# Linear attention and a Strassen-like MLP on one core: order at the changes of chunk, loads spread out, a last transpose on TensorE

## The chip, the core and the metric

The program runs on one core of a Trainium2 chip. The metric is the device time of one execution in microseconds (us). A core has five instruction streams that run beside each other and meet at semaphores: TensorE (PE, with its weight loads PEld), VectorE (DVE), ScalarE (ACT), GpSimd (POOL) and SyncE (SP), which here only issues transfers (SPq in the views is its queue). Each stream is executed in order, so an instruction that waits holds up all that stand behind it.

## What is computed

```
phi(x)  = exp(h - max h) / sqrt(128),  h = (x*s) @ omega.T - |x*s|^2/2
x       = phi(q) @ (phi(k).T @ v) / (phi(q) @ sum phi(k) + 1e-6)   # 8 batches, 8 heads, 576 x 64
u       = x + (x.T @ U @ V).T                                       # x as 8 x 576 x 512, rank 32
out     = u + relu(u @ w1) @ w2                                     # 512 -> 2048 -> 512
```

All of it is in float32. For precision each factor of a product of the MLP is split into a high part (rounded to the matmul's own float type) and a low part (what the rounding lost), and three passes are summed: high*high, high*low, low*high.

## The kernel before

The program has two halves. The first, up to some 306 us, is the attention and the rank-32 mixing; it leaves u in DRAM. The second is the MLP over 36 tiles of 128 rows, six to a **chunk** (768 rows), so six chunks, 0 to 5. Chunk 0 is computed plainly. Chunk 1 uses seven products in place of eight for the first matrix product (`products`). Chunks 2 to 5 do so for both (`products2` and `Group`).

**A pair.** The 2048 hidden columns go in eight pairs `p` = 0 to 7. In a pair, `product(i)` for i = 0 to 6 is six matmuls of 384 columns, summed in one of two PSUM banks: X for even i, Y for odd i. After product i, `after(i)` lists copies and sums that combine the seven into hidden values, apply the relu and split them. A step of the schedule is one i, and n = 7p + i counts 0 to 55 through a chunk. The next pair takes the same two banks with the names exchanged: its product 0 writes the old Y, its product 1 the old X. So product 1 of a pair waits until everything that reads X in step 6 of the pair before is done. The last reader of X is the low part of its relu, `less(T[2] ...)` at line 1063 (chunks 2 to 5), or the second instruction of `relu` at line 999 (chunk 1).

**The second product.** From pair 2 of chunk 2 on, each step also has on PE a block of the second matrix product of the two pairs before (`Group.block(s)`, line 1293, s = 0 to 13 over two pairs), six matmuls, whose result `evict` adds on DVE to a sum in SBUF (line 816). In chunks 0 and 1 the second product is plain (line 1136), its matmuls put between the products by `take`.

**Order.** Nearly all of the second half is pinned to the order in which the code issues it (`keep`). `between(i)` issues, after each step, the transfers (`feed` loads the weights `wx` of the products six steps ahead, `group.load` and `done.load` those `wy` of the second product) and the preparation of the next chunk by `forward`: `fetch` loads a quarter of 128 columns of u (96 KB, line 376), `turn` transposes 32x32 blocks on DVE into `w1f` (line 952), `prepare` forms the four sums of blocks (the fourth on POOL, line 816, the others on DVE, line 806), `add` copies one operand to its high part on ACT (line 978) and puts its low part (DVE, line 806) into `later`, from where `lowers()` issues it one step later. In chunk 1, `new.add` and `pairs.add` prepare the weights of the next pair (lines 806, 809, 813) and `seconds` those of the second product (`wa`, `wb`, `wt`, lines 806, 816, 897, 898). `stores` holds the additions of u and the writes of the plain second product (lines 1162, 1163). `leave` writes the chunk before out: `turn_out` transposes a quarter on DVE, `write_out` (line 1322) stores it in 128-byte pieces. At the end of the program `end` does the same for the last chunk.

## Time and profile before

| | |
|---|---|
| runs | 1071.74, 1068.39, 1064.89 us; median 1068.39 |
| profiled execution | 1066.96 us, its span from first to last instruction 1065.2 us |
| PE busy | 1036.5 us, 97% of the span |
| DVE, ACT, POOL busy | 785.2, 600.8, 478.5 us |
| mean granted TensorE clock | 0.995 of full speed |
| DMA | 226.45 MB, mean 213 GB/s; 326720 of 389027 packets under 512 bytes |

PE is busy nearly all the time, so only the moments at which it stands still, and the end, are of interest. A bracket behind a row gives the idle time of the row's engine just before it, and what ended it. The second half begins at about 440 us (chunk 1), 574 us (chunk 2), and then a chunk every 118 us.

### The profile page before, as it was taken

To read this page: it belongs to the slowest core of one execution; us is meant where nothing else is said; L and a number is where in the kernel's file an instruction comes from. 1 tells how busy PE (TensorE), PEld (TensorE's weight loads), DVE (VectorE), ACT (ScalarE), POOL (GpSimd) and SP (SyncE) were. 2 spreads that over 40 slices of the span, in tenths; PEclk is the share of its full clock that TensorE was granted. 3 is DMA by queue.
4 is the path that set the end of the run, shared out by engine and by line. 5 is a ranking of instruction groups with operands and counts; after the bars stand their busy time and mean duration, and the time that the engine had idled before them with its cause. 6 is when DMAs were issued, how large, how long until landed. Compare 5 with 4: busy or idle time off the path is not lost.

```text
span 1065.2 us, 19235 instructions
## 1 busy us (share of the span) xinstructions
PE 1036.5 (97%) x6447; PEld 990.4 (93%) x6447; DVE 785.2 (74%) x1546; ACT 600.8 (56%) x1497; POOL 478.5 (45%) x419
## 2 busy tenths in 40 slices
PE   8999999999999999999998999999999999999996
PEld 7899999999989999889887999999999999999995
DVE  4798998998977776576766567776678667876555
ACT  5889989998856664444444433543445333543430
POOL 3346537557445555477863323422334223433221
PEclk9999999999999999999999999999999999999998
DMA  9899989788224475298877999789997999888886
GB/s 136 145 164 146 181 178 165 154 179 131 90 78 151 146 161 98 91 321 267 260 249 266 317 242 284 250 262 283 283 302 246 284 272 306 251 267 273 256 230 139
DMA packets 389027, 226.45 MB, mean 213 GB/s; under 512 B 326720, under 2 KB 341056, under 8 KB 388928
## 3 DMA queue, kind: packets, MB, share of 16 engines
q1 hardware_dynamic: 380160, 224.13, 80.6%
q10 hardware_dynamic: 8768, 1.08, 0.7%
q8 instruction: 52, 0.85, 0.4%
q14 instruction: 47, 0.39, 0.1%
HBM read 176.91 MB, written 48.23 MB: 211 GB/s over the span
## 4 chain that ended last, share of the span: by engine, by line
PE 86%; DVE 7%; ACT 3%; DMA 2%; issue 1%; POOL 1%; DVEq 0%; SPq 0%; ACTq 0%; POOLq 0%
PE p_s L1017 24%; PE p_c L1293 11%; PE p_o L1293 6%; PE p_p L990 6%; PE p_kv L486 4%; PE p_n L532 4%; PE p_n L1136 4%; PE p_q L1136 4%; PE p_p L574 3%; PE p_r L1293 3%; PE p_p L575 3%; PE p_p L576 3%; PE p_q L512 2%; PE py L346 2%; PE p_kv L1136 2%; PE p_m L1136 2%
## 5 line engine op out<-in xcount | busy, mean ns | idle before, releaser
L1017 PE MATMUL p_s<-ux,wx 128*128 128x384 f32 x1680 | 338.9, 337 | 8.8 <-DVE t L1063 6.4
L1017 PEld LDWEIGHTS p_s<-ux,wx 128*128 128x128 f32 x1680 | 297.9, 189 | 17.3 <-DVE t L1063 8.0
L589 ACT ACTIVATE e<-p_p,nm 128x128 f32<-128x128 f32 x576 | 167.0, 389 | 24.1 <-DVE nm L582 15.8
L1293 PE MATMUL p_c<-t,wy 128*128 128x384 f32 x768 | 153.6, 335 | 3.3 <-DVE w1f L816 1.9
L816 POOL TENSOR_TENSOR near<-b,near 128x384 f32<-128x384 f32 x32 | 42.6, 1331 | 252.4 <-DVE near L1063 252.4
L436 POOL TENSOR_TENSOR xl<-xT,xh 128x384 fp32r<-128x384 f32 x95 | 94.1, 1010 | 112.9 <-ACT xh L432 91.6
L1293 PEld LDWEIGHTS p_c<-t,wy 128*128 128x128 f32 x768 | 134.6, 188 | 5.2 <-DVE w1f L816 3.2
L582 DVE TENSOR_REDUCE nm<-p_p 128x4 f32<-128x512 f32 x144 | 97.9, 680 | 23.2 <-PE p_p L576 12.7
L1073 ACT CAST t<-near 128x768 fp32r<-128x768 f32 x64 | 53.6, 838 | 95.9 <-DVE near L1063 82.3
L574 PE MATMUL p_p<-omh,xh 128*128 128x256 f32 x288 | 92.7, 322 | 1.1 <-ACT e L589 0.9
L816 DVE TENSOR_TENSOR near<-p_s,near 128x384 f32<-128x384 f32 x88 | 48.7, 553 | 46.9 <-PE p_s L1017 42.7
L575 PE MATMUL p_p<-oml,xh 128*128 128x256 f32 x288 | 81.6, 283 | 0.0
L576 PE MATMUL p_p<-omh,xl 128*128 128x256 f32 x288 | 81.5, 284 | 0.0
L1293 PE MATMUL p_o<-t,wy 128*128 128x384 f32 x384 | 76.5, 334 | 0.0
L816 POOL TENSOR_TENSOR t<-near,t 128x768 fp32r<-128x768 f32 x32 | 61.7, 1930 | 31.2 <-ACT t L1073 31.2
L532 PE MATMUL p_n<-kv,eT 128*128 128x65 f32 x512 | 71.3, 269 | 0.1
L990 PE MATMUL p_p<-ux,wx 128*128 128x384 f32 x384 | 70.7, 335 | 0.0
L532 PEld LDWEIGHTS p_n<-kv,eT 128*128 128x128 f32 x512 | 67.1, 192 | 2.3 <-DVE x L557 0.3
L990 PEld LDWEIGHTS p_p<-ux,wx 128*128 128x128 f32 x384 | 67.6, 188 | 1.6
L1293 PEld LDWEIGHTS p_o<-t,wy 128*128 128x128 f32 x384 | 67.5, 188 | 0.0
L486 PE MATMUL p_kv<-vt,e 128*128 128x65 f32 x480 | 66.3, 262 | 0.6 <-ACT e L589 0.6
L183 POOL TENSOR_TENSOR mag<-mag,low 128x512 int32<-128x512 int32 (+2 forms) x35 | 45.3, 1295 | 46.2 <-DVE mag L161 42.6
(176 smaller groups left out, 2244.6 us busy)
## 6 DMA issues: line engine op xcount, KB each, us to landing
wx<-wx_dram SPq DMA_DIRECT2D x112, 512.0 KB, 4.7
wy<-w2x_dram SPq DMA_DIRECT2D x112, 512.0 KB, 5.2
raw<-in_moe_w_ch_dram SPq DMA_DIRECT2D x32, 512.0 KB, 4.3
wx_dram<-wx SPq DMA_DIRECT2D x56, 256.0 KB, 2.4
u_dram<-x SPq DMA_DIRECT2D x36, 256.0 KB, 2.2
qt<-in_q_dram SPq DMA_DIRECT2D x120, 72.0 KB, 2.9
uraw<-u_dram SPq DMA_DIRECT2D x80, 96.0 KB, 6.5
kt<-in_k_dram SPq DMA_DIRECT2D x52, 144.0 KB, 5.0
```

The costliest lines, as they stand in the source:

```text
L486: tc.keep_in_program_order(nc.tensor.matmul(o, e[:, j, :], w, start=(s == 0 and j == 0), stop=(s == NT - 1), skip_group_check=True))
L532: nc.tensor.matmul(pn[:, h, :], eT[:, h, :], kv[:, h, s // 5, :], start=True, stop=True)
L574: nc.tensor.matmul(o, part.xh[g][:, ts], oh, start=True, stop=False)
L575: nc.tensor.matmul(o, part.xh[g][:, ts], ol, start=False, stop=False)
L576: nc.tensor.matmul(o, part.xl[g][:, ts], oh, start=False, stop=True)
L582: nc.vector.tensor_reduce(out=self.nm[:, :n], in_=self.pp[:, :n], axis=AX.X, op=ALU.max, negate=True)
L589: nc.scalar.activation(out=self.e[:, j, :], in_=self.pp[:, j, :], func=AF.Exp, bias=self.nm[:, j : j + 1])
L816: keep(engine.tensor_tensor(out=out, in0=a, in1=b, op=op))
L990: keep(nc.tensor.matmul(ph, l, r, start=(cc + i == 0), stop=(cc == NC - 1 and i == 2)))
L1017: keep(nc.tensor.matmul(o, l, r, start=(i in (0, 1, 3) and k + j == 0), stop=(k == 1 and j == 2), skip_group_check=True,))
L1136: keep(nc.tensor.matmul(po, l, r, start=(begin and n + i == 0), stop=(end and n == len(fs) - 1 and i == 2)))
L1293: keep(nc.tensor.matmul(bank, l, r, start=(fresh and n + m == 0), stop=(n == 1 and m == 2), skip_group_check=True,))
```

## The change

It is made of five parts. (1) In `products2` the low part of X's relu and its reader come ahead of the copy and the sum of the double tile `t75`, on ACT and on DVE, and behind the eviction of the step's block. (2) In `products` the low parts of the relus go into a list and are issued a step later, behind the sum of that step; at step 6, behind `between(6)`. (3) At the changes of chunk the `add`s, the `prepare`s and the weight sums are dealt out over other steps. (4) The loads of u for a chunk are issued every second step, the first half of them in the chunk before the one before; the outputs leave in quarter tiles of 48 KB from four rooms that are used twice a chunk. (5) At the end, the last two quarters are transposed by TensorE, copied out of PSUM by ACT and DVE, and stored in pieces of 1 KB by six transfers of SP. The core of the diff:

```diff
     def relu(self, x, due=None):
         g = gp.tile([P, 2, HT], F32R, name="g", bufs=6)
         keep(nc.scalar.activation(out=g[:, 0], in_=x, func=AF.Relu))
-        keep(nc.vector.scalar_tensor_tensor(
+        step = lambda: keep(nc.vector.scalar_tensor_tensor(
             out=g[:, 1], in0=x, scalar=0.0, in1=f32(g[:, 0]), op0=ALU.max, op1=ALU.subtract
         ))
+        step() if due is None else due.append(step)
...
         for i in range(7):                                     # products
             self.product(i, w(i), (X, Y))
             take(steps, spread[i])
+            old = len(due)
             after(i)
+            for _ in range(old):
+                due.pop(0)()
             lowers()
             between(i)
+        for step in due:
+            step()
...
             elif i == 5:                                       # products2
                 sums(c12, Y, u2, ADD)
                 flush()
                 less(c22, c12, c22)
                 less(c12, c12, b11)
                 sums(two[0], b11, c22, SUBTRACT, nc.gpsimd)
-                due.append(both(7, 5, c_2, nc.vector))
             elif i == 6:
                 keep(nc.scalar.activation(out=two[1], in_=X, func=AF.Relu))
                 one(2, X)
-                flush()
+                due.append(both(7, 5, c_2, nc.vector))
...
             evict()
-            if i < 5:
-                for _ in range(early_due):
-                    due.pop(0)()
+            for _ in range(early_due if i < 5 else len(due)):
+                due.pop(0)()
...
             while nxt.made < NC:                               # end of chunk 0
                 nxt.add()
                 lowers()
+            nxt.prepare(4)
...
+    SECOND = (
+        tuple(b + a for b in (8, 16, 22, 28) for a in range(4)), (15, 21, 27, 33), (36, 37, 43), tuple(range(49, 56)),
+    )
...
-                    if i == 0:                                 # chunk 1
+                    if i in (0, 1, 2):
+                        now.add()
+                    if i == 2:
                         pairs.add()
-                    if i == 1:
-                        now.prepare(4)
-                    if i in (0, 2, 3):
-                        now.add()
-                for _ in range((0, 0, 0, 1, 2, 2, 2)[i] if p == 0 else 1):
+                if p == 1 and i < 3:
+                    pairs.add()
+                for _ in range((0, 0, 0, 1, 1, 1, 1)[i] if p == 0 else (0, 1, 1, 1, 1, 1, 2)[i] if p == 1 else 1):
                     if new:
                         new.add()
...
-                forward(nxt, n, ((8, 16, 22, 28), (15, 21, 27, 33), (36, 38, 40), (50, 51, 52, 53, 54, 55)))
-                if n == 53:
+                forward(nxt, n, SECOND)
+                if n == 52:
                     nxt.prepare(4)
...
-    ADDS, REST = (50, 51, 52, 55), (0, 1, 2)
+    EARLY_U = (46, 48, 50, 52, 54, 56, 58, 60)
+    LATE_U = tuple(range(24, 40, 2))
+    TURNS, SUMS, ADDS, REST = (22, 23, 36, 44), (25, 45, 46), (49, 50, 51, 55), (0, 1, 2)
+    OUT_A = {8: (2, 0), 9: (2, 1), 10: (3, 0), 11: (3, 1)}
+    OUT_B = {21: (4, 0), 24: (4, 1), 28: (5, 0), 32: (5, 1)}
+    WRITE_B = (29, 31, 33, 34, 36, 38, 40, 41, 43, 45, 47, 48, 50, 52, 54, 55)
...
-                    forward(nxt, n, ((20, 24, 30, 34), (29, 33, 38, 42), (35, 43, 44), ADDS))
-                    if n == 53:
+                    forward(nxt, n, (LATE_U, TURNS, SUMS, ADDS))
+                    if n == 52:
                         nxt.prepare(4)
+                    if c == 2 and n in range(4, 20, 2):
+                        nxt.fetch((n // 2 - 2 & 3,))
+                    elif c > 2 and n + 56 in EARLY_U:
+                        nxt.fetch((EARLY_U.index(n + 56) % 4,))
+                if second_next and n in EARLY_U:
+                    second_next.fetch((EARLY_U.index(n) % 4,))
...
+                if n in OUT_A or n in OUT_B:                   # leave
+                    k = (*OUT_A, *OUT_B).index(n)
+                    ys[k] = half_room(k % 4)
+                    turn_out(c - 1, *(OUT_A.get(n) or OUT_B[n]), ys[k])
+                k, a = divmod(n - 12, 4)
+                if 0 <= k < 4:
+                    write_out(c - 1, 2 + k // 2, k % 2, a, ys[k])
...
+    last = [half_room(2 + j) for j in range(2)]                # the end
     for s in range(14):
...
+        if s > 11:
+            done.evict(4, j, parted(done.banks[1, j]), parted(last[j]))
...
+    for half in (1, 0):
+        y = dec.tile([P, 2 * DM], F32, name="near", tag="raw", bufs=RB)[:, :TOK].rearrange("p (t m) -> p t m", t=3)
+        for t in range(3):
+            po = ps.tile([P, 2 * P], F32, name="p_t", tag="p_p", bufs=2)
+            for j in range(2):
+                x = sum_of(NCH - 1, 5, j).rearrange("p a b -> p (a b)") if half else last[j]
+                keep(nc.tensor.transpose(po[:, j * P : (j + 1) * P], x[:, t * P : (t + 1) * P], ident))
+            if (t + half) % 2:
+                keep(nc.scalar.copy(out=y[:, t], in_=po))
+            else:
+                keep(nc.vector.tensor_copy(out=y[:, t], in_=po))
+            r = first[NCH - 1] * P + half * HT + t * P
+            keep(nc.sync.dma_start(out=rows_out[r : r + P, 2 * P :], in_=y[:, t]))
```

How the instructions stand, at three places. First, DVE at the end of pair 0 of chunk 2 (`near` are the copies and sums in SBUF, `t_8124` is t75, `t_8133` the low part of X's relu). Before:

```order
L816 TENSOR_TENSOR near<-p_s,near 128x384 x2
L1063 SCALAR_TENSOR_TENSOR t_8109<-near,t_8109 128x384
L1063 SCALAR_TENSOR_TENSOR near<-near 128x384
L1063 SCALAR_TENSOR_TENSOR near<-near,b_8012 128x384
L816 TENSOR_TENSOR t_8124<-near,t_8124 128x2x384
L1063 SCALAR_TENSOR_TENSOR t_8133<-p_s,t_8133 128x384
L1162 TENSOR_TENSOR u<-p_q,u 128x512
```

With the change, at the same place:

```order
L816 TENSOR_TENSOR near<-p_s,near 128x384 x2
L1069 SCALAR_TENSOR_TENSOR t_8109<-near,t_8109 128x384
L1069 SCALAR_TENSOR_TENSOR near<-near 128x384
L1069 SCALAR_TENSOR_TENSOR near<-near,b_8014 128x384
L1069 SCALAR_TENSOR_TENSOR t_8133<-p_s,t_8133 128x384
L816 TENSOR_TENSOR t_8135<-near,t_8135 128x2x384
L1166 TENSOR_TENSOR u<-p_q,u 128x512
```

The reader of X (`<-p_s`) has moved one row up, past the subtraction of t75, which needs ACT's copy of `near`.

Second, DVE at the end of pair 3 of chunk 1 (`g<-p_s` is the last reader of X there). Before:

```order
L816 TENSOR_TENSOR near<-p_s,near 128x384
L999 SCALAR_TENSOR_TENSOR g<-near,g 128x384
L999 SCALAR_TENSOR_TENSOR g<-p_s,g 128x384
L806 SCALAR_TENSOR_TENSOR wt<-wa,wb 128x256
L806 SCALAR_TENSOR_TENSOR wt<-wt,wa 128x256
L952 STREAM_TRANSPOSE w1f<-uraw 128x384 x2
```

With the change:

```order
L816 TENSOR_TENSOR near<-p_s,near 128x384
L999 SCALAR_TENSOR_TENSOR g<-near,g 128x384 x2
L806 SCALAR_TENSOR_TENSOR wt<-wa,wb 128x256
L806 SCALAR_TENSOR_TENSOR wt<-wt,wa 128x256
L952 STREAM_TRANSPOSE w1f<-uraw 128x384 x2
L999 SCALAR_TENSOR_TENSOR g<-p_s,g 128x384
```

Here the reader of X has moved down, past two sums of weights and two transposes.

Third, SP in pairs 0 and 1 of chunk 2. Before:

```order
L1353 DMA wx<-wx_dram 128x1024 x2
L1163 DMA out_dram<-u 128x512
L1353 DMA wx<-wx_dram 128x1024
L1275 DMA wy<-w2x_dram_5402 128x1024
L1163 DMA out_dram<-u 128x512
```

With the change:

```order
L1361 DMA wx<-wx_dram 128x1024
L376 DMA uraw<-u_dram_69 32x24x32
L1361 DMA wx<-wx_dram 128x1024
L1167 DMA out_dram<-u 128x512
L376 DMA uraw<-u_dram_69 32x24x32
L1361 DMA wx<-wx_dram 128x1024
L1280 DMA wy<-w2x_dram_5402 128x1024
L376 DMA uraw<-u_dram_69 32x24x32
```

A load of u has come in at every second step, between the loads of weights.

## Rows read from the trace of the kernel before

**Rows 1.** PE's waits: engine, line, for whom; us in total, times, longest us.
```profile
PE p_s L1017 <- DVE t L1063: 6.4, 5, 2.8
PE p_c L1293 <- DVE w1f L816: 1.9, 4, 1.0
PE p_s L1017 <- DVE ux L806: 1.1, 1, 1.1
PE p_s L1017 <- DVE g L999: 1.1, 1, 1.1
PE p_n L1136 <- ACT g L998: 0.9, 1, 0.9
```
**Rows 2.** Windows: us, busy us (count) of PE, PEld, DVE, ACT, POOL; clock, DMA share, GB/s.
```profile
586.00:590.00 4.00, 4.00 (x16) 4.00 (x17) 1.75 (x4) 2.36 (x4) 1.97 (x2) 0.61 0.67 202
590.00:594.00 4.00, 4.00 (x24) 3.95 (x23) 2.29 (x5) 1.53 (x3) 0.00 (x0) 0.97 0.92 296
640.00:660.00 20.00, 18.34 (x103) 17.38 (x102) 13.23 (x25) 7.62 (x15) 8.28 (x5) 1.00 1.12 253
660.00:680.00 20.00, 20.00 (x118) 20.00 (x117) 13.16 (x23) 10.08 (x18) 4.51 (x3) 1.00 0.89 318
680.00:700.00 20.00, 19.10 (x109) 18.46 (x108) 17.94 (x28) 9.75 (x17) 6.70 (x4) 1.00 0.71 230
```
**Rows 3.** Timeline at the end of pair 3 of chunk 1: start, us, engine, instruction.
```profile
501.08 0.56 DVE L999 SCALAR_TENSOR_TENSOR g<-p_s,g 128x384 fp32r<-128x384 f32 x1 [0.29 <-ACT g L998]
...
502.68 0.94 DVE L806 SCALAR_TENSOR_TENSOR wt<-wa,wb 128x256 f32<-128x256 f32 x1 [1.03 <-POOL wb L816]
...
503.89 1.23 PE L1017 MATMUL p_s<-ux,wx 128*128 128x384 f32 x6
...
504.43 1.03 DVE L952 STREAM_TRANSPOSE w1f<-uraw 128x384 f32<-128x384 f32 x2
```
**Rows 4.** Timeline at the ends of pairs 0 and 1 of chunk 2.
```profile
582.88 0.56 DVE L1063 SCALAR_TENSOR_TENSOR near<-near,b 128x384 f32<-128x384 f32 x1
...
583.47 0.83 ACT L1073 CAST t<-near 128x768 fp32r<-128x768 f32 x1 [1.81 <-DVE near L1063]
...
584.84 1.31 POOL L816 TENSOR_TENSOR near<-near 128x384 f32<-128x384 f32 x1 [0.54 <-ACT near L1100]
...
585.21 0.55 DVE L1063 SCALAR_TENSOR_TENSOR t<-p_s,t 128x384 fp32r<-128x384 f32 x1
585.68 0.68 DVE L1162 TENSOR_TENSOR u<-p_q,u 128x512 f32<-128x512 f32 x1
...
585.82 9.16 PE L1017 MATMUL p_s<-ux,wx 128*128 128x384 f32 x42 [2.80 <-DVE t L1063]
...
586.83 0.37 SPq L1353 DMA_DIRECT2D wx<-wx_dram  x1
...
597.79 1.31 PE L1017 MATMUL p_s<-ux,wx 128*128 128x384 f32 x6 [1.77 <-DVE t L1063]
```
**Rows 5.** All loads of wx (L1353): from issue to landing.
```profile
DMA to landing us min/median/max: 3.4/4.7/10.7
```
**Rows 6.** Timeline at the change from chunk 2 to 3.
```profile
683.22 1.84 POOL L816 TENSOR_TENSOR w1f<-w1f 128x768 f32<-128x768 f32 x1 [7.28 <-DVE ux L806]
683.52 1.95 DVE L1063 SCALAR_TENSOR_TENSOR t<-near,t 128x384 fp32r<-128x384 f32 x1
```
**Rows 7.** Timeline of the end.
```profile
1041.69 1.32 PE L1293 MATMUL p_c<-t,wy 128*128 128x384 f32 x6 [0.98 <-DVE w1f L816]
...
1051.18 4.33 PE L1293 MATMUL p_c<-t,wy 128*128 128x384 f32 x24
...
1056.85 5.75 ACTq L1322 DMA_DIRECT2D out_dram<-yh  x8
```
**Rows 8.** All stores of line 1322: from issue to landing.
```profile
DMA to landing us min/median/max: 1.7/4.7/8.2
```
**Rows 9.** The attention's transposes on PE (L512): ns min/median/max, first and last start.
```profile
L512 PE MATMUL p_q<-ident,e x288: 270/273/332, 30.8 to 303.3; 128*128 128x128 f32 x144
```

More of the change, by code (lines that the diff above doesn't have):

```diff
@@ L994, in whole1, with relu @@
             return g
-        def relu(self, x):
+        def relu(self, x, due=None):
             g = gp.tile([P, 2, HT], F32R, name="g", bufs=6)
             keep(nc.scalar.activation(out=g[:, 0], in_=x, func=AF.Relu))
-            keep(nc.vector.scalar_tensor_tensor(
+            step = lambda: keep(nc.vector.scalar_tensor_tensor(
                 out=g[:, 1], in0=x, scalar=0.0, in1=f32(g[:, 0]), op0=ALU.max, op1=ALU.subtract
             ))
+            step() if due is None else due.append(step)
             return g
@@ L1025, in products @@
             y5, c11, _ = self.room()
-            g = {}
+            g, due = {}, []
             def after(i):
@@ L1032, in after @@
                     sums(c11, Y, p1, ADD)
-                    g[0, 0] = self.relu(c11)
+                    g[0, 0] = self.relu(c11, due)
                 elif i == 2:
@@ L1039, in after @@
                     sums(c22, X, y5, ADD)
-                    g[1, 1] = self.relu(c22)
+                    g[1, 1] = self.relu(c22, due)
                 elif i == 5:
                     sums(c12, Y, u2, ADD)
-                    g[0, 1] = self.relu(c12)
+                    g[0, 1] = self.relu(c12, due)
                 elif i == 6:
-                    g[1, 0] = self.relu(X)
+                    g[1, 0] = self.relu(X, due)
             for i in range(7):
@@ L1296, in block, with evict @@
             return lambda: self.evict(i, j, parted(bank))
-        def evict(self, i, j, bank):
+        def evict(self, i, j, bank, to=None):
             if i == 2 and self.g < LAST:
@@ L1305, in evict @@
             else:
-                sums(a, bank, a, ADD)
+                sums(to or a, bank, a, ADD)
     def turn_out(c, i, j, y):
@@ L1333, in forward @@
     def forward(new, n, at):
-        base, turn, prepare, add = at
-        for j, b in enumerate(base):
-            if b <= n < b + 4:
-                new.fetch((n - b,))
+        pieces, turn, prepare, add = at
+        if n in pieces:
+            new.fetch((pieces.index(n) % 4,))
         if n in turn:
@@ L1354, in feed @@
             wq[q], wq[q + 1] = pair[:, 0], pair[:, 1]
+    chunks = {c: Chunk(c) for c in range(2, NCH)}
     for c in range(1, 2):
-        now, nxt = nxt, Chunk(c + 1)
+        now, nxt = nxt, chunks[2]
         second_weights = (None for p in range(NH) for _ in seconds(p))
@@ L1393, in performer_mlp_kernel @@
             steps = now.second([p, p + NH], g, p == 0, p == NH - 1)
-    ADDS, REST = (50, 51, 52, 55), (0, 1, 2)
+    EARLY_U = (46, 48, 50, 52, 54, 56, 58, 60)
[4 more added lines that the diff above has]
+    WRITE_B = (29, 31, 33, 34, 36, 38, 40, 41, 43, 45, 47, 48, 50, 52, 54, 55)
     pend, done = [], None
     for c in range(2, NCH):
-        now, nxt = nxt, Chunk(c + 1) if c + 1 < NCH else None
+        now, nxt, second_next = chunks[c], chunks.get(c + 1), chunks.get(c + 2)
         now.res, ys = {}, {}
@@ L1422, in between @@
                         stores.pop(0)()
-                    if n == 0:
-                        now.add()
                 elif n in REST:
@@ L1429, in between @@
                 if nxt:
[L1430 to L1431 removed]
+                    forward(nxt, n, (LATE_U, TURNS, SUMS, ADDS))
+                    if n == 52:
                         nxt.prepare(4)
[L1434 to L1449 removed]
+                    if c == 2 and n in range(4, 20, 2):
[4 more added lines that the diff above has]
+                    second_next.fetch((EARLY_U.index(n) % 4,))
+            def leave(n):
+                if n in OUT_A or n in OUT_B:
[5 more added lines that the diff above has]
+                    write_out(c - 1, 2 + k // 2, k % 2, a, ys[k])
+                if n in WRITE_B:
+                    k, a = divmod(WRITE_B.index(n), 4)
+                    write_out(c - 1, 4 + k // 2, k % 2, a, ys[4 + k])
             at = 7 * NH * (c - 2) + 7 * p
@@ L1463, in end @@
             write_out(NCH - 1, i, j, a, y, nc.scalar if j else nc.sync)
-    ys = {}
+    last = [half_room(2 + j) for j in range(2)]
     for s in range(14):
-        done.block(s)()
+        bank = done.block(s)
+        j = s % 2
+        if s > 11:
+            done.evict(4, j, parted(done.banks[1, j]), parted(last[j]))
+        else:
+            bank()
         done.load(s)
-        j = s % 2
         if s in (6, 7):
-            ys[j] = whole_room()
-            end(2, j, ys[j][:, :HT])
-        elif s in (10, 11):
-            end(3, j, ys[j][:, HT:])
-        elif s > 11:
-            end(5, j, half_room(j))
-    for j in range(2):
-        end(4, j, half_room(2 + j))
+            end(2, j, half_room(j))
+        elif s in (9, 10):
+            end(3, 1 - j, whole_room()[:, :HT])
+    for half in (1, 0):
[7 more added lines that the diff above has]
+                keep(nc.scalar.copy(out=y[:, t], in_=po))
+            else:
+                keep(nc.vector.tensor_copy(out=y[:, t], in_=po))
+            r = first[NCH - 1] * P + half * HT + t * P
+            keep(nc.sync.dma_start(out=rows_out[r : r + P, 2 * P :], in_=y[:, t]))
 _INS = ['q', 'k', 'v', 'omega', 'moe_U', 'moe_V', 'moe_w_ch1', 'moe_w_ch2']
```

15 lines of the change are left out of this document (removed).

## The prediction

> **What bounds the kernel now.** The page comes first: PE is busy 97% of the span at a clock of 0.995, so a gain can only come from the moments at which PE stands still, and from the end, where it has nothing left. The view of PE's waits [rows 1] names them in the second half; five of these groups add up to 11.4 us. The windows [rows 2] tell what a wait really costs. An undisturbed stretch of 20 us holds 118 matmuls, 0.17 us each; the stretch with a change of chunk holds 109. Nine are missing, 1.5 us, while PE's idle time there is only 0.9 us in two waits (20.00 less 19.10). So I add 0.3 us to each wait that a row shows, for the pipeline that fills again. The timelines [rows 3, 4, 6, 7] then show, wait by wait, what ended last. In chunks 2 to 5 it is nearly always the same thing: bank X is released by the low part of its relu, and that stands on DVE behind other work.
>
> **The change, place by place.** Minus is a gain.
>
> *Start of chunk 1: -2.6.* PE waited 1.1 us for a low part of an operand (`ux`) and 0.9 us for a relu on ACT that stood behind copies of weights [rows 1]; with 0.3 each, 2.6. With the change the fourth sum is issued at the end of chunk 0, the three last operands at steps 0, 1 and 2, so each low part lies at least two steps ahead of its product, and four copies of weights have left this pair. ACT's copy of the seventh operand still has to wait for POOL. Bounds 0 and -2.6; I take the upper gain, as two steps are more than the wait was.
>
> *Ends of pairs 3, 4 and 5 of chunk 1: +2.1, +1.0, -1.4.* By the second order shown, the reader of X at the end of pair 3 now stands behind two `wt` sums and two transposes. The first `wt` could not start before 502.68, since POOL's sum `wb` ended then, and the second transpose ended at 505.46 (504.43 + 1.03); another 0.56 us for the reader gives 506.0. PE began product 1 of the next pair at 503.89 [rows 3]: 2.1 us of new waiting. Bounds: 0 if the `wb` sum comes that much earlier, 2.4 with the filling pipeline. At the end of pair 4 two shorter `wt` sums stand in front; between 0 and 2.1 I take half, 1.0. At the end of pair 5 a sum of blocks leaves the queue ahead of the reader, and with it the wait of 1.1 us for `g` [rows 1], 1.4 with the filling; bounds 0 and -1.4.
>
> *Ends of pairs 0 and 1 of chunk 2: -4.0.* No blocks of the second product stand between the pairs yet, so nothing covers the chain. Before, DVE ended its last `near` at 583.44, ACT then copied t75 (to 584.30), DVE subtracted, and only then read X, from 585.21; PE went on at 585.82 [rows 4]. With the change the reader follows `near` at once: 583.45 to 584.0, so PE goes on some 1.8 us earlier. The long wait also lowered the clock: after those 2.80 us the window 586 to 590 shows 0.61 of full speed (the lower level, 1.2 in place of 2.4 GHz, for most of it) and 16 matmuls, where the next 4 us hold 24 [rows 2]: 8 x 0.17 = 1.4 us. After the wait of 1.77 us at 597.79 nothing like that is seen, and 1.0 us is left of the first wait, so I count the 1.4 as gained. The second wait, 1.77, goes almost wholly: -1.8. Against that, +1.0: SP issues the weights of step 14 only after the store of u at step 6, which waits for DVE's addition (585.68 to 586.36), and then at 586.83 [rows 4]. DVE's queue there is no shorter than it was, but PE now reaches step 14 at about 590.3 (584.0 and six products of 1.04), 3.5 us later, while these loads take 3.4 to 10.7 us, 4.7 in the median [rows 5]. 4.7 - 3.5 gives 1.2, with the load of u ahead in the queue or not; bounds 0 and 2.4; I take 1.0.
>
> *640 to 660 us, chunk 2: -2.2.* 103 matmuls in place of 118 at a DMA share of 1.12, with 1.66 us of idle time [rows 2]. The quarters of u were loaded there in every step, between the weights on SP's queue; now it is every second step, and half of them earlier. Bounds: 0, and 15 x 0.17 = 2.5 (some of the missing matmuls may be missing records).
>
> *Three changes of chunk: -4.5.* Each loses 1.5 us (one window of the three stands in [rows 2]). Two things delay the reader of X there, and both move. A low part of an operand is issued between the sums of steps 4 and 5; it now comes a step earlier. And DVE's low part at 683.52 took 1.95 us instead of 0.56, since POOL's sum in `w1f` ran from 683.22 to 685.06 [rows 6]: DVE got nothing done until POOL was through. That sum now starts a step, 2.1 us, earlier, so it ends before DVE comes to this instruction. I expect X to be free 0.9 us before PE asks: from the end of product 5, DVE needs 0.57 x 4, then the eviction of step 5, that of step 6, which cannot start before 3.1 us, and the reader, 4.3 in all; PE asks at 5 x 1.04 = 5.2. Bounds 0 and -4.5.
>
> *Before the last group: -1.3.* PE waited 0.98 us for an eviction that stood behind t75 and the reader [rows 7]; it now stands ahead of both.
>
> *The end: -3.7.* PE's last matmul ends at 1055.51 and ACT's eight last stores are issued from 1056.85 on, until 1062.60 [rows 7]; the last begins half a microsecond before that, at 1062.1. With the change six pieces pass through two PSUM banks: two transposes (0.27 us each as the attention's [rows 9], overlapping, so 0.4) and a copy of some 0.45 us (0.56 for 384 columns, here 256), ACT and DVE in turn. Two pieces per 0.95 us, three rounds: 2.85, so the last transfer is issued at 1058.4 by SP, which has done its other stores by then. Both kinds of store land in 1.7 us at best [rows 8], so the landing cancels: 1058.4 - 1062.1 = -3.7. Bounds -2.7 and -4.7: a third of a round per bank slower, or landings of the larger pieces at the shortest seen.
>
> *At nothing:* the smaller output tiles. The bytes stay, SP issues eight more stores per chunk at some 0.4 us, and it waits most of a step anyway; if that slack went, weights six steps ahead would come late first.
>
> **Here the trace and a page are weighed.** ACT's copy of t75 ended at 584.30 and POOL started its second subtraction at 584.84, held up by ACT's relu of X [rows 4]. That relu now comes first, so POOL may start at the same moment as DVE's subtraction of t75, and the rows leave open who is first; I count no wait. The Trainium skill (SBUF - State Buffer, section "Who interferes with whom") says that a DVE instruction with two SBUF inputs and a GpSimd instruction that reads SBUF exclude each other for the whole instruction, and that the one issued first goes first. The trace agrees on DVE's side, with the 1.95 us above; POOL's 1.31 us at 584.84 show no delay behind DVE's. By that rule alone the sum would be 1.2 us less of a gain.
>
> **Sum.** -2.6 + 2.1 + 1.0 - 1.4 - 4.0 - 2.2 - 4.5 - 1.3 - 3.7 = -16.6. From the profiled 1066.96 that is 1050.4; the median of the runs, 1068.39, lies 1.4 above the profiled one, so I forecast **1051.8**. With the gains at their upper bounds and the new waits at 0 it is 5.1 lower (2.1 + 1.0 + 1.0 + 1.0), 1046.7; with both new waits of chunk 1 at 2.1, the late weights at 2.4, and nothing gained at 640 us, at pair 5 and at one of the last two places, 1057.9.
>
> **Rivals.** (a) *DVE meets POOL at every pair.* If POOL goes first in all 32 pairs, t75 ends up to 1.3 us later. Mostly the 0.9 us of slack and the next step cover it, since the reader of X is through by then; at pair 0 of chunk 2 it delays the addition, the store and so the weights of step 14: +1.2, and some tenths elsewhere, **1053.4**. For it: the two become ready within 0.05 us. Against: t75 is read by PE only steps later. (b) *The reader of X is now held by the eviction.* It stands behind the eviction of step 6, and that waits for PE's block. If DVE's queue is longer than I count (it was busy 17.94 of 20 us at the change of chunk [rows 2]), the 0.9 us are used up and the gains of the three changes and of the last group stay out, 5.8: **1057.6**. (c) *New waits eat more.* If the wait at pair 3 is long enough to lower the clock (+1.4), pair 4 costs 2.1, the weights of step 14 come 2.4 us late and the stretch at 640 us gains nothing: 1.4 + 1.1 + 1.4 + 2.2 more, **1058**. (d) *Slower: the four output rooms.* Each is used twice a chunk; DVE's transpose into it waits for the stores of its first use, whose last is issued 6 steps earlier (12.5 us) in one case and 5 steps (10.4 us) in three. Stores land in 4.7 us in the median, 8.2 at most [rows 8]. Were they to need over 10.4 us, counted from the step, DVE would stand, X would stay taken, and each us beyond 0.9 would cost PE one, twelve times over chunks 3 to 5: at 13.6 us, 12 x 2.3 = 27 us, **1079**. Against it: SP keeps in step with PE, and the load on DMA is spread.
>
> **Chances.** About 1% is what this measurement can tell from no change, 10.7 us here: faster means below 1057.7. Forecast 0.58 (nearly all faster), (a) 0.14 (nearly all faster), (b) 0.12 and (c) 0.12 (each somewhat under half faster, the rest the same), (d) 0.04. That gives faster 0.78, same 0.17, slower 0.05. The range reaches from the forecast's low bound, 1046, to 1060, which takes in (a) to (c) with a little for the spread of the runs.
>
> **What would show it.** Right: the group `p_s <- DVE t L1063` of PE's waits falls from 6.4 us to about 1; the windows at the three changes hold 117 or 118 matmuls; the clock stays up at pair 0 of chunk 2; the last transfer is issued some 3 us after the last product. Wrong: new waits of PE for `g` at the ends of pairs 3 and 4 of chunk 1 of more than 3 us together (c); waits for `wx` or `wy` in chunk 2 (c); `p_s <- DVE t` after the eviction of step 6 (b); DVE idle ahead of a transpose into `yh`, ended by a DMA (d). The forecast fails as a whole if PE's matmuls per 20 us fall below 117 in stretches that were undisturbed.

## The result and the profile after

The changed kernel takes **1055.16 us** (median of 6 runs, 1053.24 to 1056.55), the kernel before beside it 1066.62 (6 runs): a ratio of 0.9887, 95% interval 0.986 to 0.9914. That is 11.5 us less; 16.6 were forecast. The profiled executions, 1066.96 and 1055.76 us, differ by 11.2, so they can be compared place by place. The table does it by the starts of the same products on PE in both timelines: how much each place made the gap larger or smaller. Minus is a gain; each measured row is rounded by itself, so the rows add up to -11.4.

| place | forecast, us | measured, us |
|---|---|---|
| everything up to the start of chunk 1 | 0 | +2.1 |
| start of chunk 1 | -2.6 | -1.6 |
| ends of pairs 3, 4, 5 of chunk 1 | +2.1, +1.0, -1.4 | +1.5, -0.1, -1.4 |
| end of pair 7 of chunk 1 | 0 | +0.7 |
| pairs 0 and 1 of chunk 2, up to step 17 | -4.0 | -1.5 |
| 640 to 660 us | -2.2 | -2.4 |
| three changes of chunk | -4.5 | -4.4 |
| before the last group | -1.3 | -1.3 |
| after the last product | -3.7 | -3.0 |
| sum | -16.6 | -11.2 |

PE's longest waits from chunk 1 on, in the columns of [rows 1] (the reader of X is at line 1069 now, `p_t` are the transposes of the end):

```profile
PE p_s L1018 <- DVE g L999: 2.2, 2, 1.3
...
PE p_s L1018 <- DVE t L1069: 0.9, 1, 0.9
...
PE p_t L1498 <- DVE near L1502: 0.8, 2, 0.5
PE p_s L1018 <- DVE b L816: 0.8, 1, 0.8
PE p_s L1018 <- ACT t L1079: 0.8, 1, 0.8
PE p_s L1018 <- ACT near L1090: 0.7, 1, 0.7
```

The 6.4 us for the reader of X are down to 0.9. Four groups for `p_s` add up to 4.5: three are new, and the one for `g`, 1.1 us at the end of pair 5 before, now stands for the ends of pairs 0 and 3. The windows, in the columns of [rows 2]:

```profile
586.00:590.00 4.00, 3.21 (x17) 2.57 (x16) 2.31 (x4) 2.44 (x6) 3.06 (x2) 1.00 0.43 100
...
640.00:660.00 20.00, 20.00 (x117) 20.00 (x116) 12.99 (x24) 8.80 (x17) 6.72 (x5) 1.00 0.96 280
680.00:700.00 20.00, 20.00 (x117) 20.00 (x116) 17.98 (x29) 11.26 (x21) 6.94 (x6) 1.00 0.98 277
```

The change of chunk and the stretch at 640 us are full now: 117 matmuls, where [rows 2] hold 109 and 103. At 586 to 590 us the granted clock stays at full speed, and yet only 17 matmuls pass, one more than at 0.61 before: PE now waits there. At the change of chunk, against [rows 6]:

```profile
678.56 1.85 POOL L816 TENSOR_TENSOR w1f<-w1f 128x768 f32<-128x768 f32 x1 [5.64 <-DVE ux L806]
...
680.65 0.55 DVE L1069 SCALAR_TENSOR_TENSOR t<-near,t 128x384 fp32r<-128x384 f32 x1
...
683.77 0.55 DVE L1069 SCALAR_TENSOR_TENSOR t<-p_s,t 128x384 fp32r<-128x384 f32 x1
...
685.18 1.20 PE L1018 MATMUL p_s<-ux,wx 128*128 128x384 f32 x6
```

POOL's sum is over before DVE needs the time (0.55 in place of 1.95 us), X is free at 684.32, and PE comes to it at 685.18 without a wait, 0.86 us later; 0.9 were forecast. The end of pair 3 of chunk 1, against [rows 3]:

```profile
502.50 0.94 DVE L806 SCALAR_TENSOR_TENSOR wt<-wa,wb 128x256 f32<-128x256 f32 x1 [1.19 <-POOL wb L816]
...
504.41 1.04 DVE L952 STREAM_TRANSPOSE w1f<-uraw 128x384 f32<-128x384 f32 x2
...
505.38 0.52 DVE L999 SCALAR_TENSOR_TENSOR g<-p_s,g 128x384 fp32r<-128x384 f32 x1
...
505.95 1.32 PE L1018 MATMUL p_s<-ux,wx 128*128 128x384 f32 x6 [1.30 <-DVE g L999]
```

The new wait is there, behind two sums and two transposes, as the order said. And pairs 0 and 1 of chunk 2, against [rows 4]:

```profile
584.68 0.55 DVE L1069 SCALAR_TENSOR_TENSOR t<-p_s,t 128x384 fp32r<-128x384 f32 x1
...
585.29 3.77 PE L1018 MATMUL p_s<-ux,wx 128*128 128x384 f32 x18 [0.94 <-DVE t L1069]
...
585.66 0.96 DVE L816 TENSOR_TENSOR t<-near,t 128x768 fp32r<-128x768 f32 x1 [0.43 <-ACT t L1079]
585.71 1.79 POOL L816 TENSOR_TENSOR near<-near 128x384 f32<-128x384 f32 x1
586.54 0.68 DVE L1166 TENSOR_TENSOR u<-p_q,u 128x512 f32<-128x512 f32 x1
587.14 0.55 DVE L816 TENSOR_TENSOR b<-p_s,near 128x384 f32<-128x384 f32 x1
587.25 0.34 SPq L1167 DMA_DIRECT2D out_dram<-u  x1
...
591.74 0.39 SPq L1361 DMA_DIRECT2D wx<-wx_dram  x1
...
598.36 1.28 PE L1018 MATMUL p_s<-ux,wx 128*128 128x384 f32 x6 [0.77 <-ACT t L1079]
...
600.80 0.56 DVE L816 TENSOR_TENSOR acc<-p_c,w1f 128x384 f32<-128x384 f32 x1 [3.65 <-DMA out_dram<-u]
601.27 0.55 DVE L816 TENSOR_TENSOR b<-p_s,near 128x384 f32<-128x384 f32 x1
```

SP issued weights at 582.29 and then stood until 587.25, since the store of step 6 waits for DVE's addition (586.54 to 587.22). The weights of step 16 went out at 591.74 and took 6.5 us, to 598.2: PE's wait at 598.36 is put down to an ACT instruction that ended then, but it fits the weights, and in the first experiment below the same wait is put down to them. At 600.80 DVE had stood 3.65 us at the first eviction, whose room is that of a tile of u. The chain of waits names the store (start, us, what):

```profile
593.23 7.47 DMA out_dram<-u
```

Behind that eviction stood the sum that reads bank Y, and PE got step 17 only at 601.87. The end, against [rows 7]:

```profile
1042.94 4.33 PE L1298 MATMUL p_c<-t,wy 128*128 128x384 f32 x24
...
1045.31 3.04 ACTq L1327 DMA_DIRECT2D out_dram<-uraw  x4
...
1047.78 0.41 DVE L1502 COPY near<-p_t 128x256 f32<-128x256 f32 x1
...
1048.39 0.70 ACT L1500 COPY near<-p_t 128x256 f32<-128x256 f32 x2 [13.71 <-DVE near L1502]
...
1048.79 2.79 SPq L1504 DMA_DIRECT2D out_dram<-near  x6
...
1050.32 0.42 DVE L1502 COPY near<-p_t 128x256 f32<-128x256 f32 x1 [0.53 <-PE p_t L1498]
```

The first of the six pieces is copied by ACT. Its wait is put down to a copy on DVE, but ACT issues stores of an earlier quarter until 1048.35 (1045.31 + 3.04), and its copy begins at 1048.39; PE's first four transposes had ended by 1047.70. SP issues its first piece when this copy is done, and then one about every 0.48 us.

### The profile page after: what moved, and what is told of

Read it like the earlier page. It is cut to its first block, busy times and chain, and to the rows that moved or that the text cites. A ratio compares the mean times of both kernels' runs of the same rounds, so it can differ in the third digit from the quotient of the medians.

```text
span 1054.0 us, 19271 instructions
## 1 busy us (share of the span) xinstructions
PE 1036.1 (98%) x6459; PEld 991.5 (94%) x6459; DVE 785.9 (75%) x1543; ACT 598.9 (57%) x1500; POOL 466.0 (44%) x419
## 4 chain that ended last, share of the span: by engine, by line
PE 85%; DVE 5%; DMA 3%; ACT 2%; SPq 2%; issue 1%; POOL 1%; ACTq 0%; DVEq 0%; POOLq 0%
PE p_s L1018 25%; PE p_c L1298 12%; PE p_p L990 6%; PE p_o L1298 6%; PE p_n L532 4%; PE p_kv L486 4%; PE p_n L1140 4%; PE p_q L1140 4%; PE p_r L1298 3%; PE p_p L574 3%; PE p_q L512 2%; PE p_p L575 2%; PE p_p L576 2%; PE py L346 2%; PE p_kv L1140 2%; PE p_m L1140 2%
## 5 line engine op out<-in xcount | busy, mean ns | idle before, releaser
L816 POOL TENSOR_TENSOR t<-near,t 128x768 fp32r<-128x768 f32 x32 | 59.1, 1848 | 38.9 <-ACT t L1079 38.9
L486 PEld LDWEIGHTS p_kv<-vt,e 128*128 128x128 f32 x480 | 63.4, 191 | 1.6 <-ACT e L589 1.5
```

The source lines that it names most:

```text
L486: tc.keep_in_program_order(nc.tensor.matmul(o, e[:, j, :], w, start=(s == 0 and j == 0), stop=(s == NT - 1), skip_group_check=True))
L816: keep(engine.tensor_tensor(out=out, in0=a, in1=b, op=op))
```

## Experiments

All medians stand beside runs of the kernel before on the same chip (medians 1065.98 to 1067.69 us). The kernels were not all run beside each other, so they are compared by their ratios to the kernel before, with the 95% interval behind, or by the stages; the intervals of the relus at once and of the last four kernels of the table overlap, so what parts these five is read from the stages. "After" is the changed kernel. The stages below, in us, are read from each kernel's profiled execution, again by the starts of products.

| kernel | start of chunk 1 | chunk 1 | chunk 2, steps 8-20 | steps 34-48 | chunk 3 to 4 | from chunk 1 to the end |
|---|---|---|---|---|---|---|
| before | 439.9 | 126.3 | 22.5 | 31.6 | 117.9 | 625.3 |
| after | 442.1 | 124.8 | 22.9 | 29.1 | 116.5 | 611.9 |
| after, again | 440.8 | 124.8 | 23.0 | 29.1 | 116.5 | 611.6 |
| relus at once | 440.5 | 122.7 | 22.9 | 29.1 | 116.5 | 609.9 |
| u as before | 441.4 | 124.8 | 22.0 | 30.1 | 116.5 | 612.3 |
| u at 14 to 21 | 439.7 | 124.9 | 20.8 | 29.1 | 116.5 | 614.0 |
| readers only | 440.0 | 126.0 | 21.8 | 32.0 | 117.6 | 620.7 |
| sum earlier | 440.3 | 126.1 | 23.0 | 29.5 | 116.5 | 621.6 |
| u spread, chunk 2 | 440.1 | 126.1 | 22.5 | 29.1 | 117.9 | 622.5 |
| store later | 440.1 | 122.9 | 20.8 | 29.1 | 116.5 | 608.1 |
| other rooms | 439.0 | 123.1 | 21.0 | 29.1 | 116.5 | 608.3 |
| reader first | 439.9 | 122.7 | 20.6 | 29.1 | 116.5 | 606.8 |
| half early | 439.3 | 122.9 | 20.9 | 29.1 | 116.5 | 607.9 |

**The relus at once** (after, one edit in `products`):

```diff
-                for _ in range(old):
+                for _ in range(old if i < 6 else len(due)):
                     due.pop(0)()
...
-            for step in due:
-                step()
```

> The changed kernel, but in chunk 1 the last low part (the reader of X) is issued straight behind step 6, ahead of the sums and transposes of that step. Theory: three waits of PE for g, at the ends of pairs 0, 3 and 7 of chunk 1, come from the reader standing behind that work; they go, 0.9 + 1.5 + 0.6 = 3.0 us, so about 1052 us, and the rows of PE's waits for g at line 999 fall from 5.9 us to under 1.5. Rival: DVE is held by POOL's sums and copies in those places whatever the order; then the waits only change their place, 1055 us.

1050.79 us, ratio 0.9857 (0.9839 to 0.9874). The waits for `g` at line 999 are gone. At the end of pair 3:

```profile
499.60 0.55 DVE L999 SCALAR_TENSOR_TENSOR g<-p_s,g 128x384 fp32r<-128x384 f32 x1
...
500.86 0.94 DVE L806 SCALAR_TENSOR_TENSOR wt<-wa,wb 128x256 f32<-128x256 f32 x1 [0.72 <-POOL wb L816]
```

The reader runs in the time in which DVE waits for POOL. Pair 0 gave 0.92, pair 3 1.47, pair 7 0.37 us: this part of the change cost time, and its undoing beats the change; its four runs (1049.51 to 1052.13) all lie below those of the change. Chunk 2 is that of the change, and here the profile puts PE's wait at step 16 down to the weights, which landed at 594.04:

```profile
594.17 1.28 PE L1018 MATMUL p_s<-ux,wx 128*128 128x384 f32 x6 [0.60 <-DMA wx<-wx_dram]
```

**Loads of u as before** (after, `forward` of chunk 2 on with the steps of before, no early loads):

```diff
-                    forward(nxt, n, (LATE_U, TURNS, SUMS, ADDS))
+                    forward(nxt, n, (ALL_U, (29, 33, 38, 42), (35, 43, 44), ADDS))
...
-                if second_next and n in EARLY_U:
-                    second_next.fetch((EARLY_U.index(n) % 4,))
```

> The changed kernel with the loads of u, the transposes and three of the sums for the next chunk back at the steps of the kernel before (no loads at steps 4 to 18 of chunk 2, none in the chunk before). Theory: the waits at steps 16 and 17 of chunk 2 (0.96 us for late weights, 1.44 us for a sum behind the late store of u) come from the eight early loads of u in that stretch; they go (-2.4), and the 2.4 us at 640 to 660 us come back: 1055 us in all, with the loss in the other place. Rival: the weights and the store are late because PE now reaches those steps 3.5 us earlier, with or without the loads; then the waits stay and the loss at 640 to 660 us is added: 1057.6 us.

1052.92, ratio 0.9889 (0.9863 to 0.9915); one of its six runs, 1060.46, lies far above the others and weighs in the ratio. Neither theory: of the waits at steps 16 and 17 only 1.0 of 2.4 us went, and of the loss at 640 us only 1.0 came back.

**Loads of u at steps 14 to 21 of chunk 2** (after):

```diff
-                    if c == 2 and n in range(4, 20, 2):
-                        nxt.fetch((n // 2 - 2 & 3,))
+                    if c == 2 and n in range(14, 22):
+                        nxt.fetch((n - 14 & 3,))
```

> The changed kernel with the eight early loads of u in chunk 2 at steps 14 to 21 in place of 4 to 18, and the second transpose and the sum that need them at steps 26 and 28. Theory: as in the run before, the waits at steps 16 and 17 go: -2.4 us, 1052.8. If eight loads in a row are too dense, as they were at 640 to 660 us of the kernel before, a new loss of 1 to 2 us appears some 6 to 10 steps later and the total is 1054 to 1055. Rival (weights late without the loads): waits stay, 1055 or more.

1055.39, ratio 0.9899 (0.9872 to 0.9925). The waits went (steps 8 to 20: 2.1 us less), but 4.2 us were lost at steps 20 to 34. The window there, in the columns of [rows 2], and SP's queue in it (start, us, instruction):

```profile
600.00:620.00 20.00, 18.12 (x101) 16.90 (x100) 11.89 (x22) 6.91 (x13) 4.17 (x3) 1.00 1.12 241
```

```profile
600.45 3.18 SPq L376 DMA_DIRECT2D uraw<-u_dram  x2
...
605.34 3.85 SPq L376 DMA_DIRECT2D uraw<-u_dram  x2
```

An issue takes up to 2 us in place of 0.4 at a DMA share of 1.12: the transfers are full, and eight loads in a row bring back what the kernel before lost at 640 us.

**Readers only** (before, with the first part of the change):

```diff
-                    due.append(both(7, 5, c_2, nc.vector))
                 elif i == 6:
...
                     one(2, X)
-                    flush()
+                    due.append(both(7, 5, c_2, nc.vector))
```

> The kernel before with one part of the change alone: in chunks 2 to 5 the reader of X ahead of the copy and the sum of t75. Theory of the prediction: at the ends of pairs 0 and 1 of chunk 2 it gains all that the whole change gains there (1.86 + 0.7 for the clock + 1.86 = 4.4 us); at the three changes of chunk only the part that the sum of t75 took, 0.96 of 1.47 us each, 2.9 us at most, since DVE's 1.95 us beside POOL's sum stay: 1066.6 - 4.4 - 2.9 + up to 1.0 for late weights = 1059 to 1060.5. Rival: the moved sum on POOL is all that matters at the changes of chunk; then 1062 to 1063.

1060.94, ratio 0.9957 (0.9943 to 0.9972). At pairs 0 and 1 it gains what the whole change gains (1.84 and 1.85 us at the two readers, and 0.71 behind the first, of which 0.5 are lost again at steps 11 and 12), and step 17 loses 1.3 without any early load of u. Each change gives 0.75 us at once, of which 0.35 is left five steps later; DVE's 1.95 us are still there:

```profile
680.89 1.84 POOL L816 TENSOR_TENSOR w1f<-w1f 128x768 f32<-128x768 f32 x1 [7.73 <-DVE ux L806]
...
681.19 1.95 DVE L1063 SCALAR_TENSOR_TENSOR t<-near,t 128x384 fp32r<-128x384 f32 x1
...
685.18 0.55 DVE L1063 SCALAR_TENSOR_TENSOR t<-p_s,t 128x384 fp32r<-128x384 f32 x1
...
686.02 1.21 PE L1017 MATMUL p_s<-ux,wx 128*128 128x384 f32 x6
```

**The sum earlier** (before, with `prepare(4)` and the operands of the next chunk one step earlier):

```diff
-    ADDS, REST = (50, 51, 52, 55), (0, 1, 2)
+    ADDS, REST = (49, 50, 51, 55), (0, 1, 2)
...
-                    if n == 53:
+                    if n == 52:
                         nxt.prepare(4)
```

> The kernel before, with two other edits of the change alone: at the changes from chunk 2 on, POOL's sum into w1f at step 52 in place of 53, and the first three operands of the next chunk at steps 49, 50 and 51 in place of 50, 51 and 52. Theory of the prediction: DVE's 1.95 us beside POOL fall to 0.56 and the reader of X comes that much earlier; with 0.75 us per change already found for the order of the readers, 0.7 us are left for these, three times: 1066.0 - 2.1 = 1064 us. Rival 1: each part alone is enough to free X in time, 1.45 each: 1061.7. Rival 2: the reader still stands behind the sum of t75, which waits for ACT, so nothing is gained: 1066.

1062.85, ratio 0.9965 (0.9951 to 0.9978). Rival 1 is right: each change gives 1.47 us, the whole of it, without the order of the readers. (POOL's sum and the operands moved together here, so the share of each is not shown; DVE's low part alone fell by 1.40 us.)

```profile
679.66 1.85 POOL L816 TENSOR_TENSOR w1f<-w1f 128x768 f32<-128x768 f32 x1 [5.20 <-DVE ux L806]
...
681.75 0.55 DVE L1063 SCALAR_TENSOR_TENSOR t<-near,t 128x384 fp32r<-128x384 f32 x1
...
685.32 0.55 DVE L1063 SCALAR_TENSOR_TENSOR t<-p_s,t 128x384 fp32r<-128x384 f32 x1
...
686.28 1.20 PE L1017 MATMUL p_s<-ux,wx 128*128 128x384 f32 x6
```

Three changes make 4.4 us, the median shows 3.2. The profiled execution lost 3.1 us between steps 39 and 43 of chunk 4, behind loads of u in a row, in a window of 100 matmuls at a DMA share of 1.12.

**Loads of u spread, in chunk 2 alone** (before):

```diff
+                    if c == 2:
+                        if n in range(4, 20, 2) or n in range(24, 40, 2):
+                            nxt.fetch((n // 2 - (2 if n < 20 else 0) & 3,))
+                        forward(nxt, n, ((), (22, 23, 36, 44), (25, 45, 46), ADDS))
```

> The kernel before, with the loads of u for chunk 3 (during chunk 2 alone) at every second step, 4 to 18 and 24 to 38, as in the change, with their transposes and sums. Theory: the 2.5 us that PE loses between steps 34 and 48 of chunk 2 come from DMA that is full there; spread out they go, and the loads at 4 to 18 cost up to 1 us at steps 16 and 17: 1066.0 - 2.5 + 0.5 = 1064. Rival: the loss there comes from DVE's transposes and sums, which move too, and has nothing to do with the loads; then it goes as well, but the windows with a DMA share over 1.1 stay.

The median, 1065.53, ratio 0.9991 (0.9976 to 1.0007), cannot tell it from no change; the interval reaches from 2.6 us gained to 0.7 lost. In the profile the 2.5 us at steps 34 to 48 are gone, with the DMA share at 640 to 660 us down from 1.12 to 0.86, and the early loads cost nothing at steps 8 to 20, where this kernel still waits for X.

**The store later, other rooms, the reader first, half early**: each on top of the one before, from the relus at once on.

```diff
-                    if n in (0, 3, 6, 9, 11, 13):
+                    if n in (0, 3, 8, 9, 11, 13):
```

> The run with the relus at once, and in chunk 2 the third addition of u and its store at step 8 in place of 6. Theory: SP stands from 582.6 to 587.3 us at that store, which waits for DVE, so the weights of steps 14 to 17 are issued late; with the store behind the weights of step 14, SP goes on issuing. The wait at step 16 goes (0.8 to 1.0 us left of it), and some 0.4 us at steps 10 to 12, where the addition stood ahead of a sum: 1050.8 - 1.3 = 1049.5 us. Rival: DMA is full in that stretch and the weights land late whenever they are issued: 1050.8, with the wait at step 16 as long.

1049.78, ratio 0.9843 (0.982 to 0.9866). Steps 8 to 20 are 2.05 us shorter: 0.75 at step 16 and 1.30 at step 17. All that is left of PE's waits from 575 to 620 us:

```profile
PE p_s L1018 <- ACT near L1088: 1.0, 1, 1.0
PE p_s L1018 <- DVE t L1067: 0.9, 1, 0.9
```

The weights of step 14 now leave SP 3.7 us earlier, before the store. Those of step 16 still go out behind the store of step 9, 6.4 us after step 8 begins as in the run before, but in the 4 us ahead of them SP issued only one load of u and two stores, where two loads of weights and a second load of u stood there too, and they land in 4.2 us in place of 6.3. The store that the first eviction waits for lands 2.05 us sooner, counted in the same way. What was expected at steps 10 to 12 only moved from step 10 to 11.

```diff
-            acc[2, j] = parted(late["rp"].tile([P, DM], F32, name="acc", tag="u", bufs=2)[:, :HT])
+            acc[2, j] = parted(dec.tile([P, DM], F32, name="acc", tag="mag", bufs=2)[:, :HT])
...
-            acc[5, j, 1] = parted(dec.tile([P, DM], F32, name="acc", tag="mag", bufs=2)[:, :HT])
+            acc[5, j, 1] = parted(late["rp"].tile([P, DM], F32, name="acc", tag="u", bufs=2)[:, :HT])
```

> The run before, and the two sums of the first blocks (the first evictions in chunk 2) in the rooms of the third and fourth tile of u in place of those of the last two. Theory: DVE stood 3.65 us at the first eviction because the room's store, issued at 593.23, landed at 600.70 us; bank Y was read late, and PE waited 1.44 us at step 17. The other rooms' stores are issued 2 to 6 us earlier, so this wait falls by 1.0 to 1.4: 1048.3 us. Rival: the eviction waits for something else (the weights of a block), or the other stores land as late: 1049.5.

1049.13, ratio 0.984 (0.9816 to 0.9863). DVE no longer stands at the first evictions (1.5 and 2.8 us in the run before), but PE had stopped waiting there: no gain by the profile.

```diff
                 elif i == 6:
+                    if early:                                  # pairs 0 and 1 of chunk 2
+                        one(2, X)
+                        flush()
+                        keep(nc.scalar.activation(out=two[1], in_=X, func=AF.Relu))
+                        less(c12, c12, b11)
+                        sums(two[0], b11, c22, SUBTRACT, nc.gpsimd)
```

> The run before, and in pairs 0 and 1 of chunk 2 the reader of X also ahead of one of the two subtractions on DVE, with ACT's relu of X ahead of its other relu. Theory: the chain that is left after the change (0.94 us of waiting at pair 0, 0.2 at pair 1) is bound by DVE; one 0.56 us instruction less in front gives 0.5 us at pair 0 and 0.2 at pair 1: 1047.6 us. Rival: POOL's sum now starts 0.6 us later, ACT's copy behind it too, and the wait at step 11 grows by as much: 1048.3.

**1048.51**, ratio 0.9834 (0.9811 to 0.9858), the lowest median of all: 0.6 us less than the run before, within the spread of its runs (1047.9 to 1049.84), and 0.4 less by steps 8 to 20. At step 8 nothing is gained: PE's wait of 0.9 us is now put down to ACT's other relu of X, which has become the last reader. Step 9 loses 0.6 us and step 11 wins 0.85, so neither theory names the place rightly.

```diff
-    for half in (1, 0):
+            pieces(13 - s)                                     # s = 12: behind the last block but one
```

> The run before, and at the end the three transposed pieces of one half between the last two blocks of the second product. Theory: the end is 3.0 us shorter than before and not 3.7 because all six pieces follow the last product and SP issues one per 0.49 us; with three of them ahead, the last is issued some 0.8 us earlier: 1046.8 us. Rival: PE's 0.65 us for the transposes delays the last block, and the copies of the last three need as long: 1047.6.

1049.1, ratio 0.9841 (0.9814 to 0.9867). The rival. The last product ends 1.4 us later, counted from the end of the one before it, and what follows is 1.2 shorter:

```profile
1040.45 0.44 PE L1493 MATMUL p_t<-ident,acc 128*128 128x128 f32 x2 [0.55 <-DVE near L1497]
...
1040.64 1.29 PE L1304 MATMUL p_c<-t,wy 128*128 128x384 f32 x6
```

The third piece waits for one of the two PSUM rooms, and the block stands behind it on PE. ACT's copy of the first piece begins at 1041.60, again right behind the last of ACT's stores (until 1041.56).

**The changed kernel again.**

> The changed kernel itself once more. Its profiled execution reached chunk 1 at 442.05 us, the latest of all profiled kernels (439.0 to 441.4 us for the same instructions). Theory: that is the spread of single executions in the first half, so this one reaches chunk 1 at 439 to 441 us, the part from there to the end takes 611.9 us again, and the median of the runs is 1053 to 1054 us. Rival: the change slows the first half by some 2 us, in a way that the order of its instructions doesn't show; then chunk 1 begins at 442 us again and the median is 1055 to 1056 us.

1054.28 beside 1067.69, ratio 0.988 (0.9861 to 0.99). The part from chunk 1 on is 611.6 us as before, and chunk 1 begins at 440.8: in the thirteen profiled executions the part up to there, whose instructions are the same, takes 439.0 to 442.1 us. In the first profile of the change the 2.1 us arise mostly at 45 to 48 us, so they are put down to the spread of single executions; the median, 0.3 us above what was expected, leaves a smaller slowing of that part possible. By the two medians the change gains 11.5 and 13.4 us.

## Why the prediction was right, and where it was 5 us off

The mechanism was right: the reader of X and POOL's sum at the changes, the spread loads at 640 us, the eviction before the last group and the shorter end gave 11.1 of the 11.7 us forecast for them. Of what was missed, 2.1 us lie ahead of chunk 1 and belong to no term; 4.9 lie in terms named below, and at pairs 3 and 4 the forecast was 1.7 us too dark, which hid part of that by luck. Step by step:

- **Start of chunk 1**: 1.0 us short. The waits for the operand and for ACT went, but the late reader of X put a new wait of 0.9 us at the end of pair 0, which the relus at once removed. The prediction looked at pairs 3 and 4 for it and missed pair 0 and pair 7 (0.7 more, of which the relus at once gave back 0.37).
- **Ends of pairs 3, 4, 5**: 0.6 and 1.1 too dark, the third exact.
- **Pairs 0 and 1 of chunk 2**: the step that failed, 2.5 us. Both readers came at once (1.86 twice, 1.8 forecast), and the weights were late by 1.0, at step 16 in place of 14. But the term for the clock, 1.4, came to 0.2: the clock stayed up, and the slow matmuls had covered a DVE sum and an ACT copy that PE then waited for (steps 10 to 12). And no term stood for step 17, 1.4 us: DVE at an eviction into a room whose store had not landed. The store later shows the common cause, SP behind DVE for 4.6 us: with that store out of the way, both waits go.
- **640 to 660 us**: as forecast in the profiled executions: the loss is there in all four profiled kernels that load u in every step at that place (2.5, 1.0, 2.9 and 0.4 us), and in none of the eight that load it in every second step. In most of these the transposes and sums moved with the loads; u at 14 to 21, where eight loads moved with one transpose and one sum and a loss came with them, speaks for the loads. Its size varies from one execution to the next, and it can come in chunk 4 as well (3.1 in one); what decides that stays open, and by the median, spreading the loads in chunk 2 alone gained only 0.5 us.
- **Changes of chunk**: 4.4 for 4.5. Of the two causes named, POOL's sum with the operands is enough alone.
- **The end**: 0.7 short. From the last product to the last issue it took 3.9 us (1047.27 to 1051.2), 2.9 forecast; some 0.3 came back behind the last issue. The three rounds were counted with ACT free from the last product on and with nothing for SP's issues. But ACT was still issuing stores when its first copy was due (until 1048.35), and SP took 0.48 us per piece, 2.4 from the first issue to the sixth. Half early, where ACT's copy stands behind its stores too, did not mend it; no run took these stores off ACT, so how much of the 1.0 us they cost stays open.

The upper end of the prediction's sum, 1057.9, leaves out one of the terms that it names: with the 1.3 before the last group it is 1059.2, still inside the range.

Of the rivals, (b) and (d) did not come: no wait for X stands behind the eviction of step 6, and no transpose into `yh` waits for a store. (a) came in another form and cost PE nothing. POOL goes first in 30 of the 32 pairs, but in 26 of them 0.9 us ahead, and DVE's subtraction of t75 takes its usual 0.95 us; in four it takes 1.23 to 1.60. At pairs 0 and 1 of chunk 2 DVE was first by 0.05 us (585.66 at pair 0), and POOL took 1.79 us beside it, where the same subtraction takes 1.02 when DVE reads PSUM beside it:

```profile
683.34 1.02 POOL L816 TENSOR_TENSOR near<-near 128x384 f32<-128x384 f32 x1
...
685.77 1.85 POOL L816 TENSOR_TENSOR t<-near,t 128x768 fp32r<-128x768 f32 x1 [1.42 <-ACT t L1079]
685.85 2.58 DVE L806 SCALAR_TENSOR_TENSOR ux<-w1f,ux 128x768 fp32r<-128x768 f32 x1
```

Two rows on, POOL was first and DVE took 2.58 in place of 0.95 us. So the rule of the Trainium skill (SBUF — State Buffer, "Who interferes with whom"), open on POOL's side in the prediction, agrees with this trace on both sides. The 1.31 us of [rows 4], which the prediction read as no delay behind DVE, were 0.3 longer than these 1.02. The 1.2 us that the rule would have cost did not come, since DVE went first where it counted. (c) came in part: late weights at 1.0 and pair 3 at 1.5, without a fall of the clock.

## What to carry to other kernels

When a long wait goes, the next chain that it covered shows up: list what else becomes ready within the time saved, on each engine and in each queue, before counting the whole of it as gained. A transfer queue that is issued in order must not hold a store that waits for a busy engine ahead of loads that are needed soon; moving one store by two steps took 2.05 us out of the profiled execution (1.0 by the medians). Stores that a computing engine issues hold up what stands behind them in its stream: here the first copy of the end, behind stores on ACT. A low part or relu that frees a PSUM bank should be issued at once, ahead of work that itself waits for another engine.

## What the runs showed of the hardware

By an estimate from two windows, a load of u of 96 KB in 128-byte pieces costs the DMA engines about as much as 512 KB of weights. The DMA view of the kernel before at 640 to 660 and at 660 to 680 us (packets and bytes; share of 16 engines):

```profile
DMA packets 6005, 5.06 MB, mean 253 GB/s; under 512 B 4915, under 2 KB 4915, under 8 KB 6005
...
q1 hardware_dynamic: 6005, 5.06, 111.9%
```

```profile
DMA packets 1745, 6.37 MB, mean 318 GB/s; under 512 B 194, under 2 KB 194, under 8 KB 1744
...
q1 hardware_dynamic: 1744, 6.35, 88.9%
```

The second gives 0.889 x 16 x 20 / 6.35 = 45 us of engine time per MB in large packets. In the first, 4.43 MB of these make 198 of 358 us, and 160 are left for 4915 small ones: 33 ns each, 25 us for the 768 of one load of u, and 23.5 us for 512 KB of weights (an estimate from these rows, which takes large packets to cost the same in both). Two steps, 4.16 us or 67 us of engine time, need two loads of weights, 47. One load of u more makes 72, and the changed kernel at 620 to 640 us (share 1.07, 117 matmuls) keeps up with that; two make 97, and the four kernels above fell behind by 0.4 to 2.9 us. The share alone does not tell the two apart: readers only held 101 matmuls at 640 to 660 us at a share of 1.03.
